# Re-ordering the first token group of a Mamba-2 scan fused with a PReLU feed-forward block

## The chip, the cores and the metric

The kernel runs on one core of one Trainium2 chip. The time is the device time of one execution in microseconds, and the time of the kernel before is 363.09 us, the median of three runs (362.66 to 364.36). The profile is of one execution with a span of 362.8 us, at a granted TensorE clock of 0.998.

## The reference, cut to what matters

The first half is a chunked state-space scan. For each batch (4) and head (8), over 768 tokens of head size 32 with a state of size 16:

```
L   = exp(cum_i - cum_j) * causal          # products of the decays a between j and i
y   = ((C B^T) * L) x  +  exp(cum_i) * (C state)
state = exp(cum_last) * state + sum_j exp(cum_last - cum_j) B_j x_j
```

The result is laid out as 3072 tokens by 256, and goes through a feed-forward block:

```
h   = x @ w_in                             # 256 -> 2048
g   = max(h, 0) + alpha * min(h, 0)        # PReLU, one alpha per column
out = g @ w_out                            # 2048 -> 256
```

x, a, B, C and alpha are fp32. The weights come as fp64, so that the kernel also has to turn 4 MB of each into fp32 by bit operations.

## The kernel before, in words

**Tiling.** A chunk is 128 tokens; two chunks are a pair (12 pairs), four chunks are a group of 512 tokens (6 groups). Groups 1 to 5 use a Strassen-like form of the two weight products (`quad`, L979 for the first product, L954 for the second). The first group can't, because the weights arrive while it runs. It uses the plain form, and it is the stage that the change touches: everything from the start to some 83 us.

**Pieces.** The weights come in 16 pieces of 512 KB in fp64: `pieces[0]`, `[1]` and `[2]` are the first three of w_in, and then pieces of w_out (3, 5, 7, 9, 11, 13, 14, 15) and w_in (4, 6, 8, 10, 12) take turns. Each holds two tiles of 128 columns of the hidden layer. A piece passes through three engines. `convert_a`: ACT takes the exponent and mantissa part (L238), POOL clamps it (L240), ACT takes the low half (L245 or L248). `sign` and `convert_b`: DVE takes the sign (L259) and joins it (L269). `convert`: POOL adds the low half into the fp32 weight (L291). `convert_next` does the last two for the next piece in line, with `first=True` also `convert_a` of the piece two further on, and loads the piece six further on. Three sets of buffers hold pieces in conversion.

**First pairs.** `first_two` writes out by hand, instruction by instruction, the scan of pairs 0 and 1: decays by VectorE scans (L765, L712), grams (L679), products with decays (`times`, L708), added states (`added`, L688), masked states (`mask`, L695), outputs (L727, L735, then the copy to xT at L740). In between are the first two pieces and the first two `hidden_two` (L870), which compute two hidden tiles for half of the group's tokens, with PReLU in two parts: ACT multiplies by the slope (L876), DVE takes the maximum (L882).

**The loop over hidden tiles.** From f = 4 to 15, each step does `hidden(0, f)` (four matmuls at L855, ACT at L858, DVE at L859), one stage of pair 2 (f = 4 to 9) or 3 (f = 9 to 14) of the scan of the next group (`pair`), conversions, and `output(f - 4)` (eight matmuls at L893). At L855 PE takes one of two PSUM buffers named hp; a buffer is free when DVE has done the PReLU of the tile in it. A stage with grams takes an hp buffer too (`spare`). At f = 8, DVE also does two scans over the decays of the later half of the batches as rows (`rows_clamp`, `rows_scan`, `rows_out`: L372, L381, L391), for which the row load is issued at f = 5.

**Order.** All five engines are scheduled by hand: instructions run on an engine in the order in which the code gives them. So where a call stands in the code decides what waits behind it.

Of the kernel before, what the change touches and what calls it, by code (L numbers as in the profile page):

```python
# [9 lines left out]
F32 = mybir.dt.float32  # L10
# [12 lines left out]
def kernel(  # L23
# [93 lines left out]

    loads = {}

    def load_rows(i):  # L120

        rows = ld.tile([RW, Q], F32, name="rows")
        nc.sync.dma_start(out=rows, in_=a.rearrange("b h (c t) -> (b h c) t", t=Q)[i * RW : (i + 1) * RW])
        loads["r", i] = rows

    scratch = {}
# [1 line left out]
    def load_a(t, b, c, eng=nc.sync):  # L128
        first = a[b, 0:1, c * Q : (c + 2) * Q]
        eng.dma_start(out=t, in_=bass.AP(tensor=first.tensor, offset=first.offset,  # L130
                                             ap=[[S, H], [0, N], [1, 2 * Q]]))
# [8 lines left out]
    def load_pair(gp, decays=True):  # L140


        b, c = divmod(2 * gp, CPB)
        turned = gp > GC
        nat = ldx.tile([P, 3, 2, H * N], F32, name="nat")
        xt = ldx.tile([P, 2, HD], F32, name="xt")

        ap = ldx.tile([P, 2 * Q], F32, name="ap")
        if gp == 0:
            load_a(ap, b, c, nc.scalar)  # L150
        elif gp >= NB:
            rows = scratch["pf", b // 2].rearrange("(b h c) t -> b h (c t)", b=2, h=H)
            rows = rows[b % 2, :, c * Q : (c + 2) * Q]
            nc.sync.dma_start(out=ap, in_=rows.unsqueeze(1).to_broadcast([H, N, 2 * Q]))
        if gp == 0:
            load_rows(0)
            nc.sync.dma_start(out=al_n, in_=moe_alpha.rearrange("(k p) -> k p", p=P))
        abc = []
        later = []
        for k in range(2):  # L160
            ts = slice((c + k) * Q, (c + k + 1) * Q)
            for i, src in enumerate((B,) if turned else (B, C)):
                nc.sync.dma_start(out=nat[:, i, k].rearrange("p (h n) -> p h n", h=H),  # L163
                                  in_=src[b, :, ts, :].rearrange("h p n -> p h n"))

            def load_x(k=k, ts=ts):
                nc.sync.dma_start(out=xt[:, k].rearrange("p (h d) -> p h d", h=H),  # L167
                                  in_=x[b, :, ts, :].rearrange("h p d -> p h d"))

            if gp < NB:  # L170
                later.append(load_x)
            else:
                load_x()
        for load_x in later:
            load_x()
        if gp == 0:
            loads["a", 1] = prep.tile([P, 2 * Q], F32, name="a1")
            load_a(loads["a", 1], b, c + 2)
        for i, src in enumerate((B, C) if turned else ()):


            for e in range(2):
                first = src[b, e : e + 1, c * Q : (c + 2) * Q, :]
                nc.sync.dma_start(out=nat[:, 1 + e, i],
                                  in_=bass.AP(tensor=first.tensor, offset=first.offset,
                                              ap=[[2 * S * N, P // 32], [8 * N, 32], [1, 8 * N]]))
        for k in range(2 if gp >= NB else 0):
            abc.append(lda.tile([P, H * Q], F32, name="abc"))
        loads["p", gp] = nat, abc, xt, ap
        if decays:  # L190
            load_spread(gp, b, c)
# [292 lines left out]
    def pair(gp):  # L484
# [9 lines left out]
        def decays(k):  # L494

            for w in range(2):
                half_decays(k, w)
# [60 lines left out]
        def spread_c():  # L558
            for e in range(2):
                nc.scalar.mul(cz[:, e].rearrange("p k t -> p (k t)"), ct, par[:, e : e + 1])  # L560

        def c_decayed():
            nc.gpsimd.tensor_tensor(out=cd.rearrange("p k t -> p (k t)"), in0=ct, in1=pf,
                                    op=ALU.mult)
# [5 lines left out]
        if fine:  # L570
            for k in range(2):
                for w in range(2):
                    if begun_scans and (k, w) != (1, 1):
                        if (k, w) != (1, 0):
                            half_decays(*divmod(2 * k + w + 1, 2))
                    else:
                        half_decays(k, w)
                    if k == 1 and w == 1:
                        spread_c()
                        c_decayed()  # L580
                    yield
        else:
            states(added(ss_tile()))
            c_decayed()
            decays(0)
            yield
            decays(1)
            spread_c()

# [57 lines left out]
    def first_two():  # L649
# [43 lines left out]
        def mask(sm, new, ks):  # L693
            n = ks.stop - ks.start
            nc.gpsimd.tensor_tensor(  # L695
                out=sm[:, ks].rearrange("p k (g m) -> p k g m", g=2),
                in0=new[:, ks].unsqueeze(2).to_broadcast([P, n, 2, 2 * D]),
                in1=hmask.rearrange("p (g m) -> p g m", g=2).unsqueeze(1)
                .to_broadcast([P, n, 2, 2 * D]), op=ALU.mult)

        def copied(gram):
            g0 = op.tile([P, GT], F32, name="o_sb").rearrange("p (k h t) -> p k h t", k=2, h=2)
            nc.scalar.copy(out=g0, in_=gram)
            return g0

        def times(i, r, gram, eng=nc.vector):
            o = dec[1][:, :, 2 * r : 2 * r + 2] if i else by_bank[:, r]
            eng.tensor_tensor(out=o, in0=gram, in1=o, op=ALU.mult)  # L708
# [34 lines left out]
        def bn_of(gp):  # L743
            return bns.pop(gp) if gp in bns else pair_loads(gp)

        def ss():
            return ps_s.tile([P, 512], F32, name="ss")
# [16 lines left out]
        for r in range(4):  # L764
# [15 lines left out]
               for i in range(2)]  # L780
# [2 lines left out]
        g0 = copied(gram[0])  # L783
        new[0] = work.tile([P, 2, 2 * D], F32, name="state")
        nc.scalar.copy(out=new[0][:, 0], in_=dps[0][:, 0])
        sm0 = work.tile([P, 2, P], F32, name="sm")
        times(0, 0, g0, nc.gpsimd)
        mask(sm0, new[0], slice(0, 1))
        g1 = copied(gram[1])
        times(0, 1, g1, nc.gpsimd)  # L790
        convert_a(*pieces[0])
        times(0, 2, gram[2])
        times(0, 3, gram[3])
        nc.vector.scalar_tensor_tensor(out=new[0][:, 1], in0=new[0][:, 0],
# [3 lines left out]
        sp.append(spread(z1, 1, bank))  # L798
        xts[0] = xtp.tile([P, KC, GT], F32, name="xT")
        convert_a(*pieces[1])  # L800
        outputs(0, (ss(), ss()), (None, sm0[:, 0]), cd0, xt0, (1, 0), 2)
        mask(sm0, new[0], slice(1, 2))
        bn1 = bn_of(1)

        sign(*pieces[0])
        decays(0, 0, sp[0][0])
        convert_b(*pieces[0])
        decays(0, 1, sp[0][1])
        convert_next()
        slope_signs()  # L810
        sign(*pieces[1])
        decays(1, 0, sp[1][0])
        convert_b(*pieces[1])
        tp = spare()
        bc1, cz1 = turned(nat1, tp)
        cd1 = work.tile([P, 2, Q], F32, name="cd")
        nc.gpsimd.tensor_tensor(out=cd1.rearrange("p k t -> p (k t)"),
                                in0=bc1[:, 2:].rearrange("p k t -> p (k t)"), in1=pf1,
                                op=ALU.mult)
        added(dps[1], bn1, xt1)  # L820
        new[1] = work.tile([P, 2, 2 * D], F32, name="state")
        for k in range(2):
            e = (k + 1) * Q - 1
            old = new[1][:, 0] if k else new[0][:, 1]
            nc.vector.scalar_tensor_tensor(out=new[1][:, k], in0=old, scalar=pf1[:, e : e + 1],
                                           in1=dps[1][:, k], op0=ALU.mult, op1=ALU.add)
        decays(1, 1, sp[1][1])
        prelus = [hidden_two(0, 0, 0, tp)]
        gram = gram_of(bc1, cz1, [bank(2), bank(3), ss(), ss()])
        g0 = copied(gram[0])  # L830
        convert_next(first=False)
# [7 lines left out]
        prelus[0]()  # L839
        convert_next(first=False)  # L840
        prelus[1]()
        outputs(1, (bank(0), bank(1)), (sm0[:, 1], sm1[:, 0]), cd1, xt1, (0, 1), 1)
        state[0] = new[1][:, 1]
        masked[0] = sm1[:, 1]
        early[0] = 16
# [311 lines left out]
    FIRST = 4  # L1157
    first_two()
    convert_a(*pieces[3])
    convert_next(first=False)  # L1160
    hidden_two(0, 0, 2 * Q, spare())()
    rest = hidden_two(0, 2, 2 * Q, spare())
    convert_a(*pieces[4])
    rest()
    identity_bank()
    bns[2] = pair_loads(2)
    convert_next(first=False)
    in_steps = {8: 0, 10: 1, 12: 2, 14: 3}
    for f in range(FIRST, NF):
        if f in (5, 10):  # L1170
            load_pair(3 + f // 10)
        if f == 5:
            load_rows(1)
        hidden(0, f)
        if f <= 10:
            ssm(2)
        if f >= 9:
            ssm(3)
        for i in {FIRST: (5,), FIRST + 1: (6, 7)}.get(f, ()):
            convert_a(*pieces[i])  # L1180
        convert_next(first=f > FIRST)
        if f == 14:
            bns[4] = pair_loads(4)
        if f == 8:
            bns[3] = pair_loads(3)
        if f == 8:
            rows_clamp(1)
            held["pr"] = rows_scan(1)
            rows_out(1)
        output(f - FIRST)  # L1190
        if f in in_steps:
            weight_sums(wi, in_sums, 0, in_steps[f])
    early[0] = None
    token_sums(1)
    ssm(2 * GC // 2, 4)

# [92 lines left out]
```

## Time and profile before

| stage (us of the span) | length | what runs |
|---|---|---|
| 0 to 29.9 | 29.9 | pairs 0 and 1, pieces 0 to 3, four `hidden_two` |
| 29.9 to 83.0 | 53.1 | the loop over f, pairs 2 and 3, pieces 4 to 15 |
| 83.0 to 362.8 | 279.8 | groups 1 to 5 by `quad`, the rest of the outputs |

| engine | busy us | share |
|---|---|---|
| PE | 353.3 | 97% |
| DVE | 247.4 | 68% |
| POOL | 202.8 | 56% |
| ACT | 170.6 | 47% |

How to read it: PE's ends are modelled, and its matmuls overlap, so 97% doesn't say that it runs at its peak. A pause of PE is read from the distance between the starts of two matmuls. In the traces a step such as "x4" is four instructions in a row, and a bracket at the end of a row names what the engine waited for before it. Times of all other engines are of the execution alone.

### The profile page before, as it was taken

How to read it: one execution, taken by the hardware profiler on the slowest of the kernel's cores; microseconds unless marked ns; L12 is line 12 of the kernel's file. 1: busy time of each engine (PE TensorE's matmuls, PEld its weight loads, DVE VectorE, ACT ScalarE, POOL GpSimd, SP SyncE). 2: the span in 40 equal slices, each digit the busy share in tenths (PEclk: the TensorE clock that was granted, in tenths of full speed). 3: DMA queues.
4: the chain of work that ended last, by engine and by line, in shares of the span. 5: the costliest groups of instructions: out<-in, count | busy, mean ns of one | idle time of the engine just before them, and what ended most of it. 6: DMA issues, size and time to landing. Idle time of an engine off the chain costs nothing.

```text
span 362.8 us, 6726 instructions
## 1 busy us (share of the span) xinstructions
PE 353.3 (97%) x2511; PEld 288.1 (79%) x2511; DVE 247.4 (68%) x465; ACT 170.6 (47%) x367; POOL 202.8 (56%) x212
## 2 busy tenths in 40 slices
PE   8899989999999999999999999999999999999995
PEld 8676656568888888888888888888888888888884
DVE  6986888977847857867757867667867633653363
ACT  3667856624354345345345345345345345444431
POOL 4976656679847956626636526537526535443521
PEclk9999999999999999999999999999999999999999
DMA  6889999931056402003703702702611001001004
GB/s 105 186 179 291 332 213 249 189 95 58 31 121 150 108 2 59 2 2 59 172 4 56 170 10 50 179 5 49 142 46 29 2 2 29 0 3 29 0 1 88
DMA packets 111016, 31.67 MB, mean 87 GB/s; under 512 B 79288, under 2 KB 106888, under 8 KB 110984
## 3 DMA queue, kind: packets, MB, share of 16 engines
q1 hardware_dynamic: 110032, 30.92, 36.8%
q8 instruction: 20, 0.33, 0.4%
q10 hardware_dynamic: 952, 0.33, 0.4%
q14 instruction: 12, 0.10, 0.1%
HBM read 27.89 MB, written 3.34 MB: 86 GB/s over the span
## 4 chain that ended last, share of the span: by engine, by line
PE 77%; SPq 7%; DMA 6%; DVE 6%; ACT 1%; issue 1%; POOL 0%; DVEq 0%; ACTq 0%
PE bank L954 31%; PE hp L979 28%; PE ss L979 6%; PE bank L893 3%; SPq L163 3%; PE ss L636 2%; SPq L167 2%; PE ss L599 2%; DVE dec L470 2%; DMA rows<-in_a_dram 2%; DMA raw<-in_moe_w_out_dram 2%; PE hp L855 1%; DMA raw<-in_moe_w_in_dram 1%; PE ss L628 1%; DMA out_dram<-o_sb 1%
## 5 line engine op out<-in xcount | busy, mean ns | idle before, releaser
L1036 POOL TENSOR_TENSOR gt<-gt 128x512 f32<-128x512 f32 x58 | 74.2, 1280 | 21.2 <-DVE gt L964 16.4
L954 PE MATMUL bank<-gt,w_out 128*128 128x256 f32 x320 | 83.5, 381 | 0.0
L954 PEld LDWEIGHTS bank<-gt,w_out 128*128 128x128 f32 x320 | 60.1, 190 | 10.3 <-issue 2.3
L1026 POOL TENSOR_TENSOR gt<-gt 128x512 f32<-128x512 f32 x20 | 25.4, 1272 | 67.4 <-DVE gt L964 62.0
L964 DVE SCALAR_TENSOR_TENSOR gt<-hp,s_mul,gt 128x256 f32<-128x256 f32 x96 | 42.0, 479 | 29.7 <-ACT gt L962 27.5
L954 PE MATMUL bank<-gt,ws 128*128 128x256 f32 x240 | 59.5, 379 | 0.0
L962 ACT ACTIVATE gt<-hp,s_alpha 128x256 f32<-128x256 f32 x96 | 40.4, 472 | 39.6 <-PE hp L979 25.9
L954 PEld LDWEIGHTS bank<-gt,ws 128*128 128x128 f32 x240 | 45.6, 190 | 6.2
L470 DVE TENSOR_TENSOR_SCAN dec<-abc,bank 128x256 f32<-128x256 f32 x80 | 48.4, 659 | 0.0
L979 PE MATMUL hp<-xs,w_in 128*128 128x256 f32 x160 | 41.9, 384 | 0.0
L979 PE MATMUL hp<-xs,ws 128*128 128x256 f32 x160 | 41.1, 379 | 0.0
L1005 DVE TENSOR_TENSOR hp<-hp,u 128x512 f32<-128x512 f32 x20 | 13.9, 697 | 29.1 <-ACT u L1003 29.1
L979 PEld LDWEIGHTS hp<-xs,ws 128*128 128x128 f32 x160 | 30.4, 190 | 4.1
L979 PEld LDWEIGHTS hp<-xs,w_in 128*128 128x128 f32 x160 | 29.7, 190 | 4.6 <-issue 0.2
L893 PE MATMUL bank<-w_out,gt 128*128 128x256 f32 x128 | 31.0, 384 | 0.0
L893 PEld LDWEIGHTS bank<-w_out,gt 128*128 128x128 f32 x128 | 23.7, 190 | 6.4 <-issue 3.1
L979 PE MATMUL ss<-xT,w_in 128*128 128x256 f32 x96 | 24.7, 380 | 0.2 <-DVE state L526 0.2
L855 PE MATMUL hp<-xT,w_in 128*128 128x512 f32 x48 | 22.8, 597 | 1.8 <-DVE gt L859 1.6
L529 POOL TENSOR_TENSOR sm<-state,bmask 128x256 f32<-128x256 f32 (+1 forms) x10 | 6.2, 621 | 29.4 <-DVE state L526 29.3
L994 ACT COPY m<-hp 128x512 f32<-128x512 f32 x8 | 4.7, 586 | 37.6 <-PE hp L979 37.6
L1003 ACT COPY u<-hp 128x512 f32<-128x512 f32 x20 | 11.7, 586 | 20.0 <-PE hp L979 20.0
L979 PE MATMUL hp<-xT,ws 128*128 128x256 f32 x80 | 20.5, 379 | 0.0
(178 smaller groups left out, 584.2 us busy)
## 6 DMA issues: line engine op xcount, KB each, us to landing
abc<-z SPq DMA_DIRECT2D x20, 512.0 KB
raw<-in_moe_w_in_dram SPq DMA_DIRECT2D x8, 512.0 KB
raw<-in_moe_w_out_dram SPq DMA_DIRECT2D x8, 512.0 KB
xt<-in_x_dram SPq DMA_DIRECT2D x24, 128.0 KB
nat<-in_B_dram SPq DMA_DIRECT2D x38, 64.0 KB
out_dram<-o_sb SPq DMA_DIRECT2D x32, 64.0 KB
nat<-in_C_dram SPq DMA_DIRECT2D x24, 64.0 KB
ap<-pf SPq DMA_DIRECT2D x11, 128.0 KB
```

The lines of the kernel that those rows point to most:

```text
L163: nc.sync.dma_start(out=nat[:, i, k].rearrange("p (h n) -> p h n", h=H), in_=src[b, :, ts, :].rearrange("h p n -> p h n"))
L470: nc.vector.tensor_tensor_scan(out=dv[:, k, hs], data0=abc[k][:, hs], data1=ident_p[0], initial=0.0, op0=ALU.mult, op1=ALU.add)
L855: nc.tensor.matmul(hp, w_in[:, k, f * P : (f + 1) * P], xts[g][:, k], start=(k == 0), stop=(k == KC - 1))
L893: nc.tensor.matmul(pos[0][t // 2][:, t % 2], gt[:, t * Q : (t + 1) * Q], w_out[:, f], start=(f == 0 and t % 2 == 0), stop=(f == NF - 1), s ...
L954: nc.tensor.matmul(ms[g][i][:, h], w, blocks[g, z][n][:, p], start=(q == 0 and h == 0), stop=(q == NQ - 1), skip_group_check=True)
L962: nc.scalar.mul(o[:, p], h[:, p], s_alpha[:, fs[p]])
L964: nc.vector.scalar_tensor_tensor(out=o[:, p], in0=h[:, p], scalar=s_mul[:, fs[p]], in1=o[:, p], op0=ALU.mult, op1=ALU.max)
L979: nc.tensor.matmul(to[:, p], w(2 * z + p), b, start=start and p == 0, stop=True, skip_group_check=True)
L1003: nc.scalar.copy(out=u2, in_=A)
L1005: nc.vector.tensor_tensor(out=Y, in0=Y, in1=u2, op=ALU.add)
L1026: nc.gpsimd.tensor_tensor(out=tc_, in0=g22, in1=g12, op=ALU.subtract)
L1036: eng.tensor_tensor(out=o, in0=x0, in1=x1, op=ALU.subtract)
```

## The change

It re-orders the first 83 us, with almost no work added or taken away:

1. The first load of the decays (`ap`, 128 KB) is issued by SyncE and the small row load by ScalarE, the other way round than before.
2. In `first_two`: the masks of the two states get tiles of their own; `convert_a` of piece 0 comes before POOL's second `times`; the second mask, the `bn` of pair 1 and the slopes' constants come after piece 0's last step; `hidden_two` of tiles 0 and 1 comes before the added states of pair 1.
3. After `first_two`: the sign of piece 3 and the PReLU of the third `hidden_two` come before the rest of piece 3.
4. In the loop, a table `CONVERTED` says at which f, before or after the scan's stage, a piece is begun (a string) or ended (a number). Most pieces are begun one or two steps later than before; piece 11, of w_out, is ended at f = 9 instead of 10; piece 7 is ended at f = 7 instead of 6.
5. The row scans go from f = 8 to f = 14.
6. `spread_c` (two ACT instructions, L560) goes from the stage before the grams to one stage earlier.
7. The added states of pair 4, at the start of the quads, go to the free half of a bank that holds the identity, instead of a buffer named ss.

```diff
-            load_a(ap, b, c, nc.scalar)
+            load_a(ap, b, c)
...
-            load_rows(0)
+            load_rows(0, nc.scalar)
...
             c_decayed()
+            spread_c()
             decays(0)
             yield
             decays(1)
-            spread_c()
...
-        sm0 = work.tile([P, 2, P], F32, name="sm")
+        sm0 = [prep.tile([P, 1, P], F32, name=f"sm{k}") for k in range(2)]
         times(0, 0, g0, nc.gpsimd)
-        mask(sm0, new[0], slice(0, 1))
+        mask(sm0[0], new[0], slice(0, 1))
         g1 = copied(gram[1])
+        convert_a(*pieces[0])
         times(0, 1, g1, nc.gpsimd)
-        convert_a(*pieces[0])
...
-        mask(sm0, new[0], slice(1, 2))
-        bn1 = bn_of(1)
-
         sign(*pieces[0])
         decays(0, 0, sp[0][0])
         convert_b(*pieces[0])
         decays(0, 1, sp[0][1])
         convert_next()
-        slope_signs()
-        sign(*pieces[1])
-        decays(1, 0, sp[1][0])
-        convert_b(*pieces[1])
         tp = spare()
         bc1, cz1 = turned(nat1, tp)
+        bn1 = bn_of(1)
+        mask(sm0[1], new[0], slice(1, 2))
+        slope_signs()
...
+        decays(1, 0, sp[1][0])
+        sign(*pieces[1])
+        convert_b(*pieces[1])
+        prelus = [hidden_two(0, 0, 0, tp)]
         added(dps[1], bn1, xt1)
+        decays(1, 1, sp[1][1])
...
-        decays(1, 1, sp[1][1])
-        prelus = [hidden_two(0, 0, 0, tp)]
...
     convert_a(*pieces[3])
+    sign(*pieces[3])
+    hidden_two(0, 0, 2 * Q, spare())()
     convert_next(first=False)
-    hidden_two(0, 0, 2 * Q, spare())()
...
+    CONVERTED = {(4, 1): ("5", 5), (5, 1): ("6", 6), (6, 1): ("7",), (7, 0): ("8", 7), (7, 1): (8,),
+                 (8, 1): ("9", 9, "10"), (9, 1): (10, "11", 11), (10, 1): ("12",),
+                 (11, 1): (12, "13"), (12, 1): (13, "14"), (13, 1): (14, "15"), (14, 1): (15,)}
...
-        for i in {FIRST: (5,), FIRST + 1: (6, 7)}.get(f, ()):
-            convert_a(*pieces[i])
-        convert_next(first=f > FIRST)
+        for steps in (CONVERTED.get((f, 0)), None, CONVERTED.get((f, 1))):
+            if steps is None:
+                if f <= 10:
+                    ssm(2)
+                if f >= 9:
+                    ssm(3)
+            for i in steps or ():
+                if isinstance(i, str):
+                    convert_a(*pieces[int(i)])
+                else:
+                    convert_next(first=False)
         if f == 14:
             bns[4] = pair_loads(4)
-        if f == 8:
-            bns[3] = pair_loads(3)
-        if f == 8:
             rows_clamp(1)
             held["pr"] = rows_scan(1)
             rows_out(1)
+        if f == 8:
+            bns[3] = pair_loads(3)
...
+    beside[GC] = m5_bank[0][:, : 2 * Q]
     token_sums(1)
     ssm(2 * GC // 2, 4)
```

More of the change, by code (lines that the diff above doesn't have):

```diff
@@ L118, with load_rows @@
     loads = {}
-    def load_rows(i):
+    def load_rows(i, eng=nc.sync):
         rows = ld.tile([RW, Q], F32, name="rows")
-        nc.sync.dma_start(out=rows, in_=a.rearrange("b h (c t) -> (b h c) t", t=Q)[i * RW : (i + 1) * RW])
+        eng.dma_start(out=rows, in_=a.rearrange("b h (c t) -> (b h c) t", t=Q)[i * RW : (i + 1) * RW])
         loads["r", i] = rows
@@ L695, in mask @@
             nc.gpsimd.tensor_tensor(
-                out=sm[:, ks].rearrange("p k (g m) -> p k g m", g=2),
+                out=sm.rearrange("p k (g m) -> p k g m", g=2),
                 in0=new[:, ks].unsqueeze(2).to_broadcast([P, n, 2, 2 * D]),
@@ L800, in first_two @@
         convert_a(*pieces[1])
-        outputs(0, (ss(), ss()), (None, sm0[:, 0]), cd0, xt0, (1, 0), 2)
-        mask(sm0, new[0], slice(1, 2))
-        bn1 = bn_of(1)
+        outputs(0, (ss(), ss()), (None, sm0[0][:, 0]), cd0, xt0, (1, 0), 2)
         sign(*pieces[0])
@@ L841, in first_two @@
         prelus[1]()
-        outputs(1, (bank(0), bank(1)), (sm0[:, 1], sm1[:, 0]), cd1, xt1, (0, 1), 1)
+        outputs(1, (bank(0), bank(1)), (sm0[1][:, 0], sm1[:, 0]), cd1, xt1, (0, 1), 1)
         state[0] = new[1][:, 1]
@@ L1174 @@
         hidden(0, f)
[L1175 to L1178, printed above, removed]
-        for i in {FIRST: (5,), FIRST + 1: (6, 7)}.get(f, ()):
-            convert_a(*pieces[i])
-        convert_next(first=f > FIRST)
+        for steps in (CONVERTED.get((f, 0)), None, CONVERTED.get((f, 1))):
[9 more added lines that the diff above has]
+                    convert_next(first=False)
         if f == 14:
             bns[4] = pair_loads(4)
-        if f == 8:
-            bns[3] = pair_loads(3)
-        if f == 8:
             rows_clamp(1)
```

## The prediction

> **What bounds the kernel now.** I read the table by stages first, then what PE waited for, then the timelines around each wait. The stages (PE, PE's weight loads, DVE, ACT, POOL, then clock, DMA share and GB/s):
>
> ```profile
> 0.00:29.86 29.86, 26.86 (x317) 21.17 (x317) 23.78 (x43) 15.75 (x33) 21.30 (x36) 1.00 0.81 162
> 29.86:47.61 17.75, 16.24 (x76) 10.14 (x77) 14.02 (x24) 13.81 (x26) 10.18 (x13) 1.00 0.99 298
> 47.61:69.62 22.01, 21.48 (x160) 13.64 (x160) 19.08 (x34) 13.49 (x24) 13.96 (x16) 1.00 0.97 244
> 69.62:82.98 13.36, 13.13 (x104) 8.38 (x105) 10.16 (x16) 4.08 (x8) 9.47 (x11) 1.00 0.43 89
> 82.98:362.80 279.82, 275.60 (x1855) 234.73 (x1855) 180.36 (x351) 123.44 (x278) 147.91 (x140) 1.00 0.24 54
> ```
>
> The last stage is PE's alone: from start to start of its matmuls I find no pause over 0.4 us in 280 us. What the first 83 us save thus arrives in the time, and nothing in the change touches the rest. How much is there? A loop step is four L855 matmuls (1.72 us in the chain of waits) and eight of L893 (1.73). Twelve steps are 41.4 us. Per pair PE also has grams (43.43 to 44.51: 1.08), outputs (74.98 to 76.37: 1.39), transposes (0.43), added states (about 0.3), together 6.4 for two pairs. So 47.8 of the 51.9 us from 29.86 to 81.74 are work, and about 4 us are lost. PE's waits from 14 to 84 us:
>
> ```profile
> PE hp L855 <- DVE gt L859: 1.6, 2, 1.1
> PE hp L688 <- DVE wr L259: 0.8, 1, 0.8
> PE ss L599 <- ACT cz L560: 0.4, 1, 0.4
> PE hp L688 <- DMA xt<-in_x_dram: 0.4, 1, 0.4
> PE ss L979 <- DVE state L526: 0.2, 1, 0.2
> PE hp L855 <- DVE gt L882: 0.2, 1, 0.2
> ```
>
> By starts these are larger: 1.27 before 47.61 and 0.69 before 69.62 (L855), 0.57 at 43.43 (L599), 0.39 at 82.98 (L979), 1.0 and 0.6 around L688. Sum 4.5 us, and that is nearly all that re-ordering can win. The largest, at 47.61, has a history:
>
> ```profile
> 37.78 0.69 ACT L238 ACTIVATE wt<-raw 128x512 f32<-128x512 f32 x1 [1.32 <-DVE gt L859]
> 39.13 0.68 ACT L238 ACTIVATE wt<-raw 128x512 f32<-128x512 f32 x1
> 41.91 0.66 ACT L858 ACTIVATE gt<-hp,s_alpha 128x512 f32<-128x512 f32 x1
> 42.61 0.75 DVE L859 SCALAR_TENSOR_TENSOR gt<-hp,s_mul,gt 128x512 f32<-128x512 f32 x1 [1.03 <-ACT gt L858]
> 46.72 0.74 DVE L859 SCALAR_TENSOR_TENSOR gt<-hp,s_mul,gt 128x512 f32<-128x512 f32 x1
> 47.61 1.96 PE L855 MATMUL hp<-xT,w_in 128*128 128x512 f32 x4 [1.11 <-DVE gt L859]
> ```
>
> At f = 5 three pieces (6, 7, 8) are begun on ACT, ahead of the PReLU of tile 6. Piece 7 is let go at 39.04 by its DMA (the chain shows its wait of 6.11 us), so ACT starts the PReLU only at 41.91, although PE had tile 6 ready near 39.6. DVE starts it at 42.61, then does 2.41 us of scans and 1.2 us of piece 7, and is late with tile 7, whose buffer the matmuls at 47.61 need. In the middle of the loop DVE also stands still for rows:
>
> ```profile
> 55.35 0.22 DVE L372 TENSOR_SCALAR r<-rows 96x128 f32<-96x128 f32 x1 [1.95 <-DMA rows<-in_a_dram]
> ```
>
> And in the first pairs POOL's order holds DVE, and PE waits for POOL's last step on piece 0 (17.33 to 18.8), behind the mask (16.32) and bn (16.73):
>
> ```profile
> 15.07 0.69 DVE L269 SCALAR_TENSOR_TENSOR wr<-wt,wr 128x512 uint32<-128x512 uint32 x1 [0.73 <-POOL wt L240]
> 17.74 0.32 PE L688 MATMUL hp<-xt,bn 128*32 128x64 f32 x8 [0.81 <-DVE wr L259]
> 18.45 0.32 PE L688 MATMUL hp<-xt,bn 128*32 128x64 f32 x8 [0.40 <-DMA xt<-in_x_dram]
> ```
>
> **What the Trainium skill says.** "Perfetto Trace Analysis", section on the per-engine timelines: ACT, DVE and GpSimd are strict FIFO, and PE's ends are estimated. The trace agrees with the first (tile 6's PReLU stands behind three conversions for 2.3 us); for the second I count starts. "SBUF — State Buffer", section "SBUF: two separate sides": VectorE and GpSimd share a port pair as a lock, and the loser waits for the whole instruction. The trace agrees in kind: L259 takes 401 to 1508 ns and L269 660 to 1792 for one shape. So moved conversions may cost up to 1 us more or less than their place suggests. "DMA: Bandwidth & Descriptors", section "Issuing engines are not separate DMA queues": issuing elsewhere only saves sequencer time. That is how I cost part 1.
>
> **The change part by part.**
>
> *Loads swapped.* ACT's issue of ap takes 1.21 us, SyncE's issue of the same shape (a, at 6.25) 0.75. So ap may land up to 0.46 sooner; DVE waited 0.34 for it at 4.28. Against it, all that SyncE issues later slips by 0.75 - 0.40 = 0.35 us, and the transposes at 7.12 need one of those loads. Between -0.3 and +0.3; I take -0.1.
>
> *First pairs.* POOL's clamp of piece 0 no longer stands behind a 1.46 us `times`, so DVE's wait of 0.73 goes. By the durations above: `times` to 12.5, mask to 12.9, clamp to 13.6, `times` to 14.9, clamp of piece 1 to 15.6; DVE has joined piece 0 by 15.1; POOL ends it near 16.9 instead of 18.8. `hidden_two` then waits for the copy of bc (16.96 + 0.59, and some 0.2 to reach PE): start 17.8 instead of 18.83. It fills the time in which PE stood for bn and xt; the added states (0.36) come after it, so the grams start at 17.8 + 1.73 + 0.36 + some 0.4 of change-over = 20.3 instead of 20.76. Then `times` on POOL ends 23.4 instead of 23.87. I take -0.45; the ends are 0 (piece 0 held by the port lock) and -0.95 (all of the 1.0 at `hidden_two` kept).
>
> *PReLU of the third `hidden_two` first.* In the trace DVE waited for ACT there (0.16 us at 28.83), not for piece 3. Nothing, and no harm: piece 3's last POOL step moves to about 30.7, the first use is at 32.09. Parts 1 and 2 shift piece 3's landing by nothing; piece 4 lands at 31.56 in both, and through POOL's chain (clamp 32.49, bn, piece 4, clamp, piece 5 ended at 38.48) holds `output(2)` to about 38.75, against 39.42 before. So at most -0.67 gets through here, and -0.55 does.
>
> *The table and `spread_c`.* Tile 6's PReLU on ACT now stands behind piece 6 alone (to about 39.1), so DVE can do it at 41.6, right after piece 6 (41.58), instead of 42.61; scans to 44.7; no conversion at f = 6, so tile 7 ends at 45.5 instead of 47.46. L855 of tile 8 then starts at about 45.6, right behind PE's own work, as the 0.57 for cz is gone too. That would be -2.0. But piece 7 is now ended at f = 7: DVE 45.5 to 46.7, POOL 46.8 to 48.1, and `output(4)` at f = 8 needs it. PE would be there at 47.4 and gets it at 48.3, against 49.41 before: **-1.1**, in which the -0.55 is contained. New wait: about 0.9 us, with all later matmuls behind it.
>
> *Rows.* At f = 8 DVE loses a stall of 1.95 and 1.5 us of work. PE did not wait there (its next pause is at 69.62), so it is worth nothing directly, but helps DVE to catch up. At f = 14 the 1.5 us lie in DVE's idle 1.87 us ahead of 80.84. SyncE's row stores now wait there too; behind them are only loads for the quads.
>
> *Pieces 8 to 15.* Ending piece 11 at f = 9 leaves f = 10 without a conversion. DVE then does tile 11 near 63.4 instead of 64.34 (before shifting), scans, piece 12, tile 12 done near 68.6 instead of 69.56; with PE earlier by 1.1 and DVE by at least as much, the 0.69 at 69.62 goes: **-0.6**. Each piece's first use is one step or more after its end.
>
> *Bank for states.* The third quad matmul no longer waits for the two state updates (82.24 to 82.84): of 0.39 I take **-0.3**.
>
> *Masks apart*: same 0.46 us on POOL, in tiles; nothing. Sum: -0.1 - 0.45 - 0.55 (up to the -1.1) - 0.6 - 0.3 = -2.0, and some -0.2 where my chains are pessimistic: 363.1 - 2.2 = **360.9 us**.
>
> **The rivals.** (A) Nearly all pauses go, because piece 7 comes in time: DVE's ops there ran at 0.42 and 0.69 us without the lock. Then -2.2 - 0.9 = -3.1, or with all of the first pairs' 0.95, -3.6: 359.5 to 360.0. Against: piece 7's chain through three engines in one step is the tightest in the table. (B) The gain is taken back by loads: DMA is at 0.97 to 0.99 from 30 to 70 us, and pieces land by it, not by order. Pieces 4 and 7 land at 31.56 and 39.04 whatever is done; if SyncE's slip of 0.35 goes through and piece 7 is later too, only parts of -0.6 and -0.3 stay: about 362.3, no measurable change. (C) Slower: with each piece begun later and ended in the same step, a lock-stretched L269 (1.79 at 58.00) or a late landing hits PE, as ACT, POOL and DVE each stand in line. Two stalls of 1.5 to 2 us over what is gained: 363.1 + 1.8 = 364.9. For it: piece 7. Against: all other pieces keep a step of slack, and DVE has 43 us of work in the 53 of the loop (second to fourth row of the stages).
>
> **How the numbers follow.** Forecast 0.48, A 0.2, B 0.22, C 0.1. The forecast is 360.9, with 0.4 to each side. The line for faster by over 0.5% is at 361.3: most of the forecast and all of A, 0.57. Same: B and the forecast's slow edge, 0.33. Slower 0.1. The range goes from A's 359.4 to 363.2, which takes in B, and leaves out C and a little.
>
> **What would show it.** Right: `hidden_two` near 17.8; no pause over 0.3 at L855 of tiles 8 and 13; a pause of about 1 us at L893 of `output(4)` for POOL's L291; L979 at once after the transposes, the last stage still 279.8 long and starting near 80.8. Wrong: ACT's L238 waiting for DMA longer than before, L893 waiting for L291 in several steps, or L870 waiting for piece 0 beyond 18.8.

## The result, and the profile after

The changed kernel takes 383.3 us (median of four runs, 381.69 to 384.49) against 363.5 in runs beside it: a ratio of 1.054, with a 95% interval of 1.049 to 1.059. The forecast was 360.9, in a range of 359.4 to 363.2. The change made the kernel 20 us slower. The profile below is of the fastest of the four runs (381.69, span 380.0, clock 0.984); in the other three PE was granted 0.975 of its clock.

The stages of the changed kernel, cut at the same places in the code as before (first group of tile 4 at 29.81, first quad matmul at 99.26; columns as before, the last three are clock, DMA share and GB/s):

```profile
0.00:29.81 29.81, 26.01 (x316) 20.55 (x317) 24.34 (x43) 15.68 (x33) 20.28 (x35) 1.00 0.84 176
29.81:47.20 17.39, 13.28 (x121) 7.81 (x121) 14.14 (x25) 8.51 (x17) 9.20 (x10) 0.99 0.98 283
47.20:66.95 19.75, 16.48 (x68) 11.17 (x65) 10.19 (x15) 11.02 (x22) 7.07 (x8) 0.85 0.83 204
66.95:99.26 32.31, 26.67 (x157) 17.07 (x156) 19.48 (x30) 10.65 (x19) 18.18 (x18) 0.94 0.13 33
99.26:380.00 280.74, 275.79 (x1857) 234.58 (x1855) 181.34 (x354) 123.62 (x278) 148.92 (x142) 1.00 0.26 58
```

In these two profiles the first pairs end at the same place (29.81 against 29.86), and the quads are 0.9 us longer. The loop over f went from 53.1 to 69.5 us. None of the other engines fills it: DVE does 43.8 us of work in it (the sum of the second to fourth rows), POOL 34.5. And in the third and fourth rows PE was granted only 0.85 and 0.94 of its clock, though it had been granted all of it before. The five largest of PE's waits, from 28 to 98 us (us in total, times, longest; L854 and L892 are what was L855 and L893 before):

```profile
PE bank L628 <- DVE dec L609: 5.6, 2, 3.7
PE ss L513 <- POOL bn L418: 3.7, 2, 2.1
PE hp L854 <- DVE gt L858: 1.8, 1, 1.8
PE bank L892 <- POOL w_out L291: 1.1, 1, 1.1
PE ss L628 <- DVE dec L609: 0.7, 1, 0.7
```

Neither of the two largest is in the list of before; the third is the wait for a PReLU that was there too (1.6 us in two). L628 is the start of a pair's outputs, L513 its added states: parts of the scan, not of the weights. PE's own timeline shows where they stand, and what follows them:

```profile
45.37 0.29 PE L628 MATMUL bank<-cd,sm 64*32 64x128 f32 x1 [1.92 <-DVE dec L609]
...
47.20 3.41 PE L892 MATMUL bank<-w_out,gt 128*128 128x256 f32 x8
...
63.18 0.43 PE L513 MATMUL ss<-xt,bn 128*32 128x64 f32 x16 [2.14 <-POOL bn L418]
63.54 3.62 PE L892 MATMUL bank<-w_out,gt 128*128 128x256 f32 x8
...
79.36 0.27 PE L628 MATMUL bank<-cd,sm 64*32 64x128 f32 x1 [3.68 <-DVE dec L609]
...
80.76 3.68 PE L892 MATMUL bank<-w_out,gt 128*128 128x256 f32 x8
```

Before, pair 2's grams started at 43.43, in the step of tile 7, and its outputs at 52.94, in that of tile 9 (first line below: the grams before; second: the outputs before; third: eight matmuls of the second product before; fourth: the grams of the changed kernel):

```profile
43.43 0.48 PE L599 MATMUL ss<-cz,bc 32*128 32x256 f32 x1 [0.41 <-ACT cz L560]
52.94 0.29 PE L628 MATMUL ss<-cd,sm 64*32 64x128 f32 x1
58.94 1.99 PE L893 MATMUL bank<-w_out,gt 128*128 128x256 f32 x8
37.62 0.48 PE L599 MATMUL ss<-cz,bc 32*128 32x256 f32 x1
```

Now the grams start at 37.6, in the step of tile 5, and the outputs are next in PE's queue at 42.3, in that of tile 6, when DVE has just begun to multiply the decays (41.63). The scan runs two stages to a step. The code says why: the loop runs over `(CONVERTED.get((f, 0)), None, CONVERTED.get((f, 1)))` and does the scan's stage at each entry that is `None`. That is the middle one, and also each of the others for which the table has no pieces. Ten of the twelve steps (4 to 6 and 8 to 14) do it twice, f = 7 once, f = 15 three times. A pair has six stages, so pair 2 is done at f = 6 and pair 3 at f = 11, and the calls in between and after find no stage left to do.

The eight L892 after each long pause take 3.4 to 3.7 us, against 1.89 to 1.99 before.

### The profile page after: what moved, and what is told of

It reads as the page before. It is cut to its first block, busy times and chain, and to the rows that moved or that the text cites. A ratio compares the mean times of both kernels' runs of the same rounds, so it can differ in the third digit from the quotient of the medians.

```text
span 380.0 us, 6723 instructions
## 1 busy us (share of the span) xinstructions
PE 358.2 (94%) x2511; PEld 291.2 (77%) x2511; DVE 249.5 (66%) x465; ACT 169.5 (45%) x367; POOL 203.6 (54%) x212
## 4 chain that ended last, share of the span: by engine, by line
PE 81%; DVE 6%; POOL 6%; ACT 2%; DMA 2%; issue 2%; SPq 1%; DVEq 0%; POOLq 0%
PE bank L953 30%; PE hp L978 27%; PE ss L978 5%; PE bank L892 5%; PE ss L636 2%; PE hp L854 2%; PE ss L599 2%; POOL w_out L291 1%; DVE dec L470 1%; PE ss L628 1%; DVE dec L609 1%; DVE gt L858 1%; DVE wr L269 1%; PE hp L869 1%; DMA out_dram<-o_sb 1%
## 5 line engine op out<-in xcount | busy, mean ns | idle before, releaser
L953 PEld LDWEIGHTS bank<-gt,ws 128*128 128x128 f32 x240 | 45.6, 190 | 6.2
L892 PE MATMUL bank<-w_out,gt 128*128 128x256 f32 x128 | 36.0, 429 | 1.1 <-POOL w_out L291 1.1
L892 PEld LDWEIGHTS bank<-w_out,gt 128*128 128x128 f32 x128 | 26.7, 214 | 9.9 <-issue 3.7
L854 PE MATMUL hp<-xT,w_in 128*128 128x512 f32 x48 | 22.8, 598 | 2.0 <-DVE gt L858 1.8
L993 ACT COPY m<-hp 128x512 f32<-128x512 f32 x8 | 4.7, 586 | 37.6 <-PE hp L978 37.6
```

Source lines behind the costliest of these rows:

```text
L854: nc.tensor.matmul(hp, w_in[:, k, f * P : (f + 1) * P], xts[g][:, k], start=(k == 0), stop=(k == KC - 1))
L892: nc.tensor.matmul(pos[0][t // 2][:, t % 2], gt[:, t * Q : (t + 1) * Q], w_out[:, f], start=(f == 0 and t % 2 == 0), stop=(f == NF - 1), s ...
L953: nc.tensor.matmul(ms[g][i][:, h], w, blocks[g, z][n][:, p], start=(q == 0 and h == 0), stop=(q == NQ - 1), skip_group_check=True)
```

## The experiments

Theory S: the stages, two to a step, make the loss. Theory L, its rival: pieces begun later by the table hold up the weights, and PE with them. Others came up on the way. The experiments were run in three groups, beside runs of the kernel before with medians of 363.09, 362.83 and 362.97, against 363.5 beside the changed kernel: a difference of times across groups can be off by up to 0.7 us.

**One stage per step, all else as changed.**

```diff
-        for steps in (CONVERTED.get((f, 0)), None, CONVERTED.get((f, 1))):
-            if steps is None:
+        for place, steps in enumerate((CONVERTED.get((f, 0)), None, CONVERTED.get((f, 1)))):
+            if place == 1:
```

> The changed kernel, but with one stage of the scan per loop step, as before: its loop over three places runs the stage at every place that holds no pieces, so twice in most steps, and this run does it at the middle place alone. Theory S (two stages per step bunch the scan's work): the 17 us lost between 30 and 98 us go, and what is left of the forecast shows: 361 us, between 359.5 and 363.5; no pause of PE at L628, no clock share under 0.95. Theory L (pieces begun later hold up the weights): the time stays over 375 us, with PE waiting for POOL's last step on pieces.

Measured: 360.87 us, ratio 0.9947 (0.9932 to 0.9962). The 22 us are gone, and what is left is the forecast to 0.1 us. Theory L alone falls. PE's waits from 28 to 100 us are one line:

```profile
PE hp L854 <- DVE gt L881: 0.2, 1, 0.2
```

The profiled execution is the slowest of this kernel's 20 (364.17): in it the first piece came late, POOL and PE waited in the first pairs, and PE ran at half its clock from 17.65 to 24.48. So I read the loop alone from it: 50.3 us from tile 4's start to the first quad matmul (32.60 to 82.89), against 53.1 before and 69.5 in the changed kernel.

**Two stages per step, on the kernel before.**

```diff
-        if f <= 10:
-            ssm(2)
-        if f >= 9:
-            ssm(3)
+        for i in range(1 if f == 7 else 2):
+            if f <= 10:
+                ssm(2)
+            if f >= 9:
+                ssm(3)
```

> The kernel before with only this added: two stages of the scan per loop step, one at f = 7, as the changed kernel does. Theory S: slower by 12 to 20 us, so 375 to 383, with PE pausing at L628 for the decays' products and at L513 for bn. Theory L: within 2 us of the kernel before, 361 to 365, as its pieces keep their places.

Measured: 372.63 us, ratio 1.028 (1.021 to 1.035). Slower by 9.5 us, with the waits that S names:

```profile
PE bank L628 <- DVE dec L609: 4.7, 2, 2.9
PE ss L513 <- POOL bn L418: 2.0, 2, 1.6
PE bank L599 <- ACT cz L560: 1.6, 1, 1.6
PE ss L599 <- ACT cz L560: 1.6, 1, 1.6
```

So S is shown, but this is less than half of 22.4, and below what I expected. The two lines of L599 are pauses for `spread_c`, one in each pair, which the changed kernel doesn't have; so its two stages must cost more elsewhere.

**The first pairs alone**, with the swapped loads, and the loop of before: parts 1 to 3 of the change.

> The kernel before with the change's first part alone: loads swapped, the new order in the first two pairs, masks apart, and the third PReLU first. The loop is that of before. The changed kernel's fifth matmul group at L854 starts at 29.81 us against 29.86 before, so both theories expect 363.3 plus or minus 0.5. My forecast on record had it 0.55 us faster. A third theory (the first pairs set back the loop through later pieces) expects over 365.

Measured: 362.78 us, ratio 0.9993 (0.9981 to 1.0005): nothing that can be told from no change, and as the interval runs from -0.7 to +0.2 us, nothing that rules out the 0.55 us of the forecast.

**The table alone**, one stage per step: the loop's edit of the first experiment on the kernel before.

> The kernel before with the table of pieces alone, one stage per step. Theory S: 361.5 to 364, since most pieces have a step of slack. Theory L: slower by over 5 us, 368 or more, with PE waiting at the second product for POOL.

Measured: 363.25 us, ratio 1.0015 (0.9998 to 1.0032). By itself the table does nothing that can be told. In its profile the pause ahead of tile 8 is gone, but the one ahead of tile 13 is 1.21 us by starts, against 0.69 before.

**Fills in the pauses, first try.**

```diff
+        if not fine:
+            keep_warm(ys[0], {2: 8, 3: 16}[gp])
...
-            states(added(ss_tile()))
+            dp = ss_tile()
+            keep_warm(dp, {2: 0, 3: 9}[gp])
+            states(added(dp))
```

> The changed kernel with matmuls on ones that no result uses put into PE's three long pauses: 8 of 256 columns before pair 2's outputs, 16 before pair 3's, 9 before pair 3's added states (0.216 us each: 1.7, 3.5 and 1.9 us, a little under the pauses of 3.0, 3.85 and 2.3). Theory K (after a long pause PE runs at half rate for a while, so that eight L892 take 3.4 to 3.7 us instead of 1.73): these three go back to 1.75 and the time falls by about 5 us, to 378. Theory W (the pauses alone are the loss): 383, plus or minus 1.

Measured: 390.27 us, ratio 1.0754 (1.0725 to 1.0783), slower still. The size was wrong, as one fp32 call of 256 columns is two records of 0.216 us; and the buffers were wrong too, since PE waited for DVE before the fill, as it had before the outputs. It decides nothing on the time. But the eight matmuls of the second product behind the first fill (at 48.79) took 1.99 us, not 3.41.

**Pieces ahead of the two stages.**

```diff
+        for steps in (CONVERTED.get((f, 0)), CONVERTED.get((f, 1))):
+            for i in steps or ():
+                ...
+        for i in range(1 if f == 7 else 2):
+            if f <= 10:
+                ssm(2)
+            if f >= 9:
+                ssm(3)
```

> The changed kernel with its two stages per step, but all pieces of a step begun and ended ahead of the two stages instead of behind them. Two stages alone cost 9.5 us on the kernel before and 22.4 in the changed one; theory Q says that the other 13 come from pieces that queue behind the bunched stages (ACT behind the copies of the outputs, POOL behind masks): 370 to 375 here. Theory R (they come from the bunched stages themselves, whose products the pieces then delay): 380 or more.

Measured: 379.75 us, ratio 1.0466 (1.0427 to 1.0505). 3.5 us come back, not 8 to 13: theory Q falls as the main cause. PE now waits longer for the decays (4.8 at most, against 3.7).

**Two stages for pair 2 only.**

```diff
+            if steps is None and (f < 9 or place == 1):
```

> The changed kernel with two stages per step for pair 2 only (f = 4 to 8), one stage for pair 3. By the starts of tile 8 (24.1 us after that of tile 4 against 16.0 with one stage) theory S expects that 8 us of the 22 come from pair 2 and stay: 369. If the loop can catch up later, 362 to 365.

Measured: 368.16 us, ratio 1.0152 (1.0115 to 1.019). Against one stage for both pairs (360.87), pair 2 costs 7.3 us and they stay, as expected; so by difference pair 3 costs the other 15. With it come the pause for bn (2.14 us in the bracket at 63.18) and the longest, for the decays (3.68 at 79.36).

**All but the table**, one stage per step.

> All of the change but the table: pieces as in the kernel before, one stage per step. My forecast put 1.1 us of its gain on the table: 362.0 here against 360.9 with it. If the table is worth nothing, as it was alone (363.25): 360.9, plus or minus 0.3.

Measured: 361.37 us, ratio 0.9963 (0.9949 to 0.9977). With the table the ratio was 0.9947 (0.9932 to 0.9962), so the table's share, 0.6 us by these ratios and give or take 0.7, can be told neither from nothing nor from the 1.1 us of the forecast. In this profile the pause ahead of tile 8 is back:

```profile
PE hp L854 <- DVE gt L858: 1.1, 1, 1.1
```

**The row scans alone**, from f = 8 to 14.

> The kernel before with the row scans alone moved from f = 8 to f = 14. My forecast gave this nothing by itself: 362.9 to 363.3. If DVE's stall of 1.95 us and its 1.5 us of work at f = 8 set PE's pause ahead of tile 13: 361.5 to 362.5.

Measured: 362.73 us, ratio 0.9992 (0.9976 to 1.0007). Nothing, as forecast. But the pause ahead of tile 13 is not in its profile, which suggests that DVE's early stall reaches that far; the 0.69 us are too little for this comparison.

**Fills in the pauses, second try**: half the calls, and a free half bank.

```diff
+            keep_warm(m5_bank[0], {2: 0, 3: 5}[gp])
             states(added(ss_tile()))
...
+        if not fine:
+            keep_warm(m5_bank[0], {2: 6, 3: 8}[gp])
```

> The changed kernel again with matmuls on ones in the three long pauses, now sized right (one call of 256 columns is two records of 0.216 us, so the fills before were twice as long as meant) and written to a half bank that nothing waits for: 6 calls (2.6 us) for the pause of 3.0, 8 (3.5) for 3.85, 5 (2.2) for 2.3. Theory K (half rate after a long pause costs 5 us): 378 to 380, and the eight L892 behind each fill take 1.75 us. Theory W (only the pauses count): 383, plus or minus 1.

Measured: 378.83 us, ratio 1.0441 (1.0412 to 1.0471): 4.5 us faster than the changed kernel, with 38 more matmul records. PE behind the last fill (L895 is the line of the second product in this kernel):

```profile
79.86 1.99 PE L895 MATMUL bank<-w_out,gt 128*128 128x256 f32 x8
```

Behind the other two fills the eight L895 take 1.99 us as well (at 46.31 and 61.24). Theory K is shown: the rate after a pause is a loss of its own, on top of the pause. The 4.5 us are what the fills give on balance, for one pause grew, from 1.76 to 3.44 us, and PE ran at half its clock from 72.36 to 75.78, behind it:

```profile
71.39 2.86 PE L857 MATMUL hp<-xT,w_in 128*128 128x512 f32 x4 [3.44 <-DVE gt L861]
```

**Two stages, without the table.**

> The changed kernel with its two stages per step, but the pieces begun and ended as in the kernel before. Two stages cost 9.5 us on the kernel before and 22.4 on the changed one. If the table's later begins make the difference (theory L as a partner of S, by how late a piece is begun, since putting the pieces ahead of the stages gave back only 3.5): 370 to 373. If the rest of the change makes it: 380 or more.

Measured: 375.46 us, ratio 1.0339 (1.0307 to 1.0371): 2.5 us over what I expected, and 7.8 below the changed kernel. So the table, whose worth with one stage can't be told from nothing, costs about 8 us with two.

**The loop's parts without the first pairs**, one stage per step.

> The change without its part on the first pairs and the loads, with one stage per step: the table, the earlier spread of C, the rows and the bank for states. By the forecast it lacks 0.45 + 0.1 us of the 360.87 of the whole: 361.4. PE's pauses ahead of tiles 8 and 13 and of the grams are gone, by all theories.

Measured: 360.95 us, ratio 0.9957 (0.9942 to 0.9971), so the first pairs add nothing that can be told. Its profile shows tiles 6 to 8 in the order that I had forecast, DVE first and then PE:

```profile
41.85 0.74 DVE L859 SCALAR_TENSOR_TENSOR gt<-hp,s_mul,gt 128x512 f32<-128x512 f32 x1
42.51 2.41 DVE L470 TENSOR_TENSOR_SCAN dec<-abc,bank 128x256 f32<-128x256 f32 x4
44.88 0.75 DVE L859 SCALAR_TENSOR_TENSOR gt<-hp,s_mul,gt 128x512 f32<-128x512 f32 x1
```

```profile
42.24 1.88 PE L855 MATMUL hp<-xT,w_in 128*128 128x512 f32 x4
...
45.13 1.99 PE L893 MATMUL bank<-w_out,gt 128*128 128x256 f32 x8
46.96 1.88 PE L855 MATMUL hp<-xT,w_in 128*128 128x512 f32 x4
```

Tile 8 starts right behind the eight L893, without the bracket that it had before. From tile 4's start (30.95) to the first quad matmul (81.23) it is 50.3 us, against 53.1 before.

## Why the prediction was wrong, point by point

**The step that failed** is in "The table and `spread_c`", and in every step that counts by f after it: I took the scan to do one stage per step, as before. I read `None` in the loop as a marker for the middle place, and did not ask what the loop does where the table has no entry. So "no conversion at f = 6, so tile 7 ends at 45.5" was right on DVE's conversions, and overlooked that the same step now held the last products and the outputs. In the sum, a term of +22.4 us was missing: 383.3 against 360.87 with one stage and the rest equal.

**What that term is made of.** A stage leaves work to DVE, ACT or POOL that the next stage's matmuls need. With one stage per step, some 3.45 us of the loop's own matmuls lie between them. With two, PE's queue holds both in a row, and the loop's matmuls come only behind the scan's: those at 47.20 behind outputs that waited for DVE until 45.37. On the kernel before this costs 9.5 us. By the medians, the rest of the 22.4 is 7.8 for the table (383.3 against 375.46), 2.8 between the two runs with two stages and no table (372.63 and 375.46), and the 2.2 by which the changed kernel with one stage is faster than the kernel before. The 2.8 is not clear of noise, as the intervals of these two ratios overlap. The half rate after long pauses, 4.5 us by the fills, is a part of these terms and does not come on top.

In the profiles, the loop of the changed kernel is 4.2 us longer than the one without the table (69.5 against 65.2); PE was also granted less of its clock in its runs (0.975 in three of four, against 0.985 to 0.990). So some of the table's 8 us is probably half rate; it was not taken apart. Why the table costs so much only with two stages is argued, not shown: when PE waits for the scan, ACT waits for PE's outputs (3.76 us at 46.89) and begins the next piece only behind the copies; DVE then stands idle for 7.17 us up to 53.08 and ends two pieces in a row, with PE waiting for the second product's weights at 56.90. Later the PReLU for which PE waits until 73.70 stands on DVE behind a piece, and POOL's clamp of that piece (71.64) comes only after two operations of the scan (68.74 to 70.30) and the end of another piece. Putting the pieces ahead of the stages gave only 3.5 us back, so their place within the step is not most of it.

**Rival C** had the sign, not the mechanism. It expected stalls on pieces that end too late; only 1.1 us of PE's waits were for a piece at L892, and without the second stage the same late pieces cost nothing that can be told (0.9947). That the result was slower, as C had it, is luck.

**The other steps**, by the runs with one stage:

- The forecast's total fits the kernel that I had priced: 360.87 and 360.95 against 360.9. That it does so to 0.1 us is partly luck, as a wait of 0.9 us in it did not come and the terms for the first pairs and the loads (-0.55) can't be seen; nor was there a line behind the last -0.2.
- The pauses ahead of tiles 8 and 13, for the grams and at L979 are all gone, 2.92 us by starts, and the gain is 2.0 to 2.2 us. The profile in which I counted them is of a run of 364.5 us, 1.4 over its median; the same loop in the kernel with the new first pairs alone has 0.9, 1.0, none and 0.4, or 2.3 in all, which is nearer to the gain. With the loop's parts alone, DVE's PReLU of tile 6 started at 41.85 (forecast 41.6), and tile 7 ended at 45.6 (forecast 45.5); but the loop of that profile starts 1.1 us later than before (30.95), so these times agree by chance. With the table alone, where tile 4 starts at 29.79, it is 40.69 and 44.5: the order was right, and the gain within the loop larger than forecast.
- The new pause of 0.9 us for piece 7 did not come. In the same profile POOL ended it at 48.53, and PE was there at 48.67. The late start of that loop is not the reason: with the table alone POOL ended it at 47.38 (forecast 48.1), and PE was there at 47.51 (forecast 47.4). It is close, with 0.1 us to spare in both, but rival A had it right.
- *First pairs*, -0.45: not found in the time, and not ruled out. Alone 0.9993 (0.9981 to 1.0005), and with the loop's parts no difference. The mechanism is there: `hidden_two` started at 17.69 in the changed kernel (forecast 17.8). Tile 4 starts at 28.64 to 29.81 in eight of the nine profiles with the new order, and at 29.02 to 29.86 in four of the five with the old one (in the other two, at 32.60 and 30.95, PE was at half its clock for a while): half a microsecond between the middles, and a spread of one. One profile of each can't show this term.
- *Loads swapped*, -0.1: PE's first work on decays started at 4.50 instead of 4.72, but POOL waited 0.63 us for the load of a, which SyncE now issues later. By 11.2 us nothing of it is left (POOL's first `times` starts at 11.17 instead of 11.22).
- *Rows*, nothing by itself: right within the interval (0.9976 to 1.0007).
- *Shared port*: L259 ran between 0.40 and 1.52 us in the changed loop too. It decided nothing here.

The best kernel of the study is the change with one stage per step, 360.87 us, by a ratio of 0.9947; without the first pairs' part no difference can be told.

## What to carry to other kernels

When a change moves calls into a loop with a table, count how often each call runs per step before pricing where it stands; a default value that is also a marker is a trap. In this pipeline, written by hand, the loop's matmuls between two stages of the scan are what hid the other engines' work: with two stages to a step, PE's waits in the changed loop went from 0.2 us in all to 13. An edit that can't be told from nothing alone (the table: 1.0015) can cost 8 us together with another, so undo parts within the changed kernel and not only on the old one. And a pause can cost more than its length, by the rate of what follows it.

## What the runs showed of the hardware

After pauses of 2.2, 2.3 and 3.9 us PE ran the same matmuls at half rate (0.43 us from start to start instead of 0.216) for about 3.4 us each time, and the granted clock over the whole profile fell from 0.998 to 0.984. Two rows of a table by stretches show it; the clock is the last number but two:

```profile
63.50:67.00 3.50, 3.50 (x18) 2.75 (x10) 2.97 (x7) 2.59 (x6) 0.01 (x1) 0.54 0.96 123
81.00:84.30 3.30, 3.30 (x9) 2.62 (x10) 0.00 (x0) 1.90 (x5) 1.37 (x2) 0.51 0.02 5
```

In steps of 0.2 us the clock is 0.50 from 46.68 to 50.10, from 63.75 to 67.16 and from 80.82 to 84.23, and 1.00 around them. Each stretch is 3.41 us long, and they begin 17.07 us apart, which is five times that length. Two other profiles fit this as well: with the pieces ahead of the stages the clock fell at 44.66 and 75.38, nine lengths apart, and with two stages and no table at 45.46 and 72.76, eight lengths apart (the later one lasted two lengths each time). So in these traces the clock changes only on a fixed grid of 3.41 us. That is why the slow stretch need not begin with the first matmul after a pause: after the one that ended at 45.37, the pairs' outputs ran at their usual rate.

Within that grid, what counts is how much of one window PE stood idle. In the loops of the seven traces with slow stretches, each of the eleven windows at full clock in which PE was idle for 1.83 us or more (by its modelled ends) was followed by one at half clock, and none in which it was idle for 1.76 us or less. So the pauses of 1.7 and 1.9 us in the changed kernel's profile, with 1.0 and 1.76 us of idle time in their windows, cost only themselves. It is not the whole rule: in the first pairs of the profile with the loop's parts alone, 1.42 us was enough.

The Trainium skill, "TensorE: Matmul & The Clock Gate", section "What's actually happening", describes a gate that halves PE's clock after an idle window of about 3.4 us and opens it after a busy window of that length, with windows that run freely. The length of the slow stretches and their grid agree; that a window idle for little more than half of its length was enough is less than the section's idle window.
